# Ranking the activation passes first, and the steps of the next block's x second, in the scheduler's order of ScalarE and VectorE

## The chip, the core and the metric

One core of one Trainium2 chip runs the kernel. A core has TensorE (PE, matmuls; PEld is its weight load), VectorE (DVE), ScalarE (ACT), GpSimd (POOL) and SyncE (SP), whose queue issues every transfer here. Each engine takes its instructions in the order in which they were built into its queue and waits on semaphores for what others make. The metric is the device time of the execution in microseconds.

## The reference, cut to what matters

```python
def phi(x):                                  # attention features, per head, 576 tokens
    proj = x @ w_phi                         # 64 -> 128
    proj = proj - max(abs(proj), axis=-1)
    return concat([exp(proj), exp(-proj)])
kv  = k_p.T @ v;  z = sum(k_p)               # q_p, k_p = phi(q), phi(k)
x   = (q_p @ kv) / (q_p @ z + 1e-6)          # to [4608 tokens, 512]
h   = x @ w_in                               # 512 -> 2048
g   = max(h, 0) + alpha * min(h, 0)
y   = g @ w_out                              # 2048 -> 512
# soft mixture: 32 slots, 8 experts
logits = y @ phi;  d = softmax over tokens;  slots = d.T @ y
out = softmax over slots (logits) @ (relu(slots @ w1) @ w2)
```

All in float32 precision. `w_in` and `w_out` arrive as 64-bit numbers and are turned to float32 on the core.

## The kernel before, in words

The 4608 tokens are 12 blocks n of 384. For each block, 16 chunks c of 128 hidden features: `gemm` (L510 to L523) makes h of the chunk in a PSUM bank with 12 matmuls of 128x384 (L520): x and w_in are each split into a high and a low part, and hi·hi, hi·lo and lo·hi are added for the four pieces of 128 of the inner dimension. In chunk 0 the eight matmuls that read `xhi` come first and the four that read `xlo` last. A bank `ph` is one of two, so the matmuls of chunk c+2 wait until chunk c was read.

`leaky` (L525 to L531) reads it: ScalarE makes relu(-h) into `gT` (L527), VectorE adds alpha_rest times that to h (L528). VectorE then transposes `gT` into `gb` (L547), and for every four chunks TensorE multiplies `gT` with the product of w_out and phi into `pl` (L556). After a block `softmax` takes the logits of the block: `pr` (L575) on TensorE, a maximum, an exponential and transposes on VectorE and ScalarE (L586 to L612), 48 or 96 small matmuls `pS` (L625), and VectorE adds those to `acc` (L644). y itself is never made: its product with the softmax weights is formed from the transposed g. The g of the first two blocks goes to HBM (`gT_d`) and comes back between chunks 4 and 15 of block 10 (`QUADS`, `reload`).

Beside the chunks of block n the attention of block n+1 runs: keys (`pk`, `kall`, `ks`, `pkv`, L269 to L366) and queries (`pq`, `pj`, `mb`, `qe`, `num`, `den`, L394 to L450). `q_finish` (L457 to L494) ends it: `recip` takes 1/den on VectorE (L462, L463) and sends it out and back over HBM so that it is spread over the partitions (L465, L470); `divide` multiplies (L486, four pieces); `scale` makes the two parts of x for the next block, `xhi` on ScalarE (L479) and `xlo` on VectorE (L480), four pieces each. There is one `xhi` and one `xlo`, so the pieces of block n+1 can be written only when the last chunk (15) of block n has read them. `conv` (L174 to L211) turns the weights to float32 until some 270 us.

`at(slot, phase, ...)` puts steps in program order around the chunks (a slot is a chunk). The order in each engine's queue is then made by a scheduler that plays the program through with its own estimate of times: of the instructions that are ready on an engine it takes the one of the highest priority, which is otherwise the place in program order. `tc.high_priority(offset=...)` moves that place ahead for what is issued inside. `combine` (L688 to L704), once per run for the first 28 groups of tokens, is a further row of VectorE passes in block 10.

Of the kernel before, what the change touches and what calls it, by code (L numbers as in the profile page):

```python
# [13 lines left out]
AF = mybir.ActivationFunctionType  # L14
ALU = mybir.AluOpType
# [46 lines left out]
def attention_prelu_softmoe(ctx: ExitStack, tc, qT, kT, v, wphi, w_in, w_out, alpha, phi, w1, w2, out):  # L62
    nc = tc.nc
# [78 lines left out]
    alpha_rest = const.tile([128, NC], F32, name="alpha_rest")  # L142
# [34 lines left out]
    def at(slot, phase, fn):  # L177
        at_step(slot, phase, fn)
# [204 lines left out]
    xhi_t, xlo_t, q_st = {}, {}, {}  # L383
# [73 lines left out]
    def q_finish(slot, n):  # L457
        st = q_st[n]

        def recip():  # L460
            rd = sm.tile([128, BT], F32, tag="dT", name="rd")[:, 0:HB]
            nc.vector.tensor_scalar(out=rd, in0=st["den"][:, 0:HB], scalar1=1e-6, scalar2=None, op0=ALU.add)  # L462
            nc.vector.reciprocal(out=rd, in_=rd)  # L463
            for j in range(2):
                nc.sync.dma_start(rc_d[n % 2][j].rearrange("p h t -> h p t"), rd[64 * j:64 * j + 64])  # L465

        def widen():
            bc = st["bc"] = xp.tile([128, NP, BT], F32, tag="bc", name="bc")
            for j in range(2):
                nc.sync.dma_start(  # L470
                    bc[64 * j:64 * j + 64], rc_d[n % 2][j, 0:NP].rearrange("p h t -> p (h t)").unsqueeze(0).to_broadcast([64, NP, BT]))

        def scale(p):
            def go():
                if p == 0:
                    xhi_t[n] = xp.tile([128, KD, BT], F32R, tag="xhi", name="xhi")
                    xlo_t[n] = xp.tile([128, KD, BT], F32R, tag="xlo", name="xlo")
                xs = st["num"][:, p, :]
                nc.scalar.copy(xhi_t[n][:, p, :], xs)  # L479
                nc.vector.tensor_tensor(out=xlo_t[n][:, p, :], in0=xs, in1=xhi_t[n][:, p, :], op=ALU.subtract)  # L480
            return go

        def divide(p):
            def go():
                xs = st["num"][:, p, :]
                ins = nc.vector.tensor_tensor(out=xs, in0=st["bc"][:, p, :], in1=xs, op=ALU.mult).ins  # L486
                tc.add_manual_dep(ins, mark[max(k for k in mark if k <= slot + 6)].name, nosync, reason="behind the load")
            return go

        at(slot, "post", recip)  # L490
        at(slot + 1, "pre", widen)
        for p in range(NP):
            at(slot + 6, "post", divide(p))
        for p in range(NP):  # L494
            at(slot + 6, "post", scale(p))
# [17 lines left out]
    def gemm(n, c):  # L513
        xhi, xlo = xhi_t[n], xlo_t[n]
        ph = ps_h.tile([128, 512], F32, tag="h", name="ph")
        h = ph[:, 0:BT]
        first = [(k, a, b) for k in range(KD) for a, b in ((0, 0), (1, 0))] + [(k, 0, 1) for k in range(KD)]
        terms = first if c == 0 else [(k, a, b) for k in range(KD) for a, b in ((0, 0), (0, 1), (1, 0))]
        for i, (k, a, b) in enumerate(terms):
            gemm_last[0] = nc.tensor.matmul(  # L520
                h, (w_in_hi, w_in_lo)[a][c][:, 128 * k:128 * k + 128], (xhi, xlo)[b][:, k, :],
                start=(i == 0), stop=(i == len(terms) - 1)).ins
        return h  # L523

    def leaky(n, c, h):  # L525
        gT = gT_t[n, c] = sm.tile([128, 512], F32, tag="gT", name="gT", bufs=5)[:, 0:BT]
        nc.scalar.activation(gT, h, AF.Relu, scale=-1.0)  # L527
        ins = nc.vector.scalar_tensor_tensor(out=gT, in0=gT, scalar=alpha_rest[:, c:c + 1], in1=h, op0=ALU.mult, op1=ALU.add).ins  # L528
        mark[NC * n + c] = ins
        if n < NDEF:  # L530
            nc.sync.dma_start(gT_d[n, c], gT)  # L531
# [216 lines left out]
    for step in range(-45, nslots + 4):  # L748
# [3 lines left out]
        h = None  # L752
        if slot is not None:
            n, c = divmod(slot, NC)
            if 0 <= slot < nslots:
                h = gemm(n, c)
# [5 lines left out]
        if h is not None:  # L762
            leaky(n, c, h)
# [69 lines left out]
    for eg in range(2):  # L833
        for j in range(4):
            nc.vector.tensor_reduce(
                out=own[:, j:j + 1], in_=ident[:, 36 * j + 16 * eg:36 * j + 16 * eg + 4], axis=AX.X, op=ALU.add)
# [3 lines left out]
    for eg in range(2):  # L840
        hr = pf.tile([128, EF], F32, tag=f"hr{eg}", name="hr")
        for fh in range(2):
            pe = ps_h.tile([128, 512], F32, tag="h", name="pe")
            for k in range(KD):
# [3 lines left out]
                out=hr[:, 512 * fh:512 * fh + 512], in0=pe, scalar1=0.0, scalar2=own[:, 4 + eg:5 + eg], op0=ALU.max, op1=ALU.min)  # L848
        t = acc[2 * eg:2 * eg + 2]
        for b in range(2):  # L850
            nc.vector.transpose(
                out=t[b].rearrange("p (b s) -> p b s", s=32),
# [115 lines left out]
```

## Time and profile before

| | |
|---|---|
| median of 3 runs (lowest to highest) | 972.08 us (970.07 to 972.95) |
| profiled execution, its own time | 973.75 us |
| its span, first to last instruction | 971.9 us |
| PE busy | 928.3 us (96%) |
| PEld / DVE / ACT / POOL busy | 654.1 / 722.1 / 443.6 / 143.5 us |
| granted TensorE clock, mean | 0.986 |
| chain of waits, by engine | PE 74%, DVE 17%, DMA 4% |

Busy times are unions over the instructions of an engine; a matmul's recorded time overlaps the next one's, so the start of one to the start of the next is what it costs. In a row of the timeline the brackets give the idle time of the engine ahead of the row and what ended it. The granted clock is 1.00 at 2.4 GHz and 0.50 at 1.2 GHz.

### The profile page before, as it was taken

The page shows a single profiled execution, that of the slowest core. Times are in us where ns is not written, and L with a number is a line of the kernel's source. Part 1 is how long each engine was busy: PE and PEld are TensorE (multiplying, and loading weights), DVE is VectorE, ACT ScalarE, POOL GpSimd, SP SyncE. Part 2 cuts the span into 40 slices and gives each one's busy share as a digit, 9 for nine tenths or more (in the row PEclk, how much of TensorE's full clock was granted, in tenths as well). Part 3 has the DMA queues.
Part 4 walks back from the last instruction along what each step waited for, and adds up shares of the span by engine and source line. Part 5 has one row for each costly group of instructions (what it writes and reads, how often), then busy time and mean ns, then how long its engine had stood idle before and what let it go on. Part 6 is the DMA issues. An engine that isn't in the chain of part 4 may idle for free.

```text
span 971.9 us, 20072 instructions
## 1 busy us (share of the span) xinstructions
PE 928.3 (96%) x8178; PEld 654.1 (67%) x8178; DVE 722.1 (74%) x1425; ACT 443.6 (46%) x867; POOL 143.5 (15%) x84
## 2 busy tenths in 40 slices
PE   6888989999989999999999999999999999899997
PEld 3446676777668676676677776776777667786454
DVE  6998999989686687677677778677756767864233
ACT  5876757766635345245335344353342341221113
POOL 4102212112112112122022112121130220000000
PEclk9898999999999999999999999999999999999999
DMA  7345655674231031031211210200212609478999
GB/s 272 119 141 177 207 169 196 213 203 122 64 87 28 23 85 43 26 78 53 51 44 42 59 53 25 75 26 23 54 34 72 177 1 302 159 268 260 311 354 335
DMA packets 75675, 122.22 MB, mean 126 GB/s; under 512 B 7872, under 2 KB 49472, under 8 KB 75584
## 3 DMA queue, kind: packets, MB, share of 16 engines
q1 hardware_dynamic: 75584, 120.95, 40.3%
q8 instruction: 64, 1.05, 0.5%
q14 instruction: 27, 0.22, 0.1%
HBM read 99.82 MB, written 21.10 MB: 124 GB/s over the span
## 4 chain that ended last, share of the span: by engine, by line
PE 74%; DVE 17%; DMA 4%; issue 2%; ACT 2%; SPq 0%; DVEq 0%; ACTq 0%
PE ph L520 37%; PE num L440 5%; PE pkv L336 5%; PE pS L625 4%; PE pl L556 4%; PE pq L407 3%; PE den L445 3%; PE pk L293 2%; PE pso L866 2%; DVE m L207 2%; DVE gT L528 1%; PE pe L846 1%; DVE mx L281 1%; PE po L902 1%; DVE rest L202 1%
## 5 line engine op out<-in xcount | busy, mean ns | idle before, releaser
L520 PE MATMUL ph<-xhi,w 128*128 128x384 f32 x1536 | 430.8, 351 | 8.2 <-ACT xhi L479 4.0
L520 PEld LDWEIGHTS ph<-xhi,w 128*128 128x128 f32 x1536 | 280.3, 189 | 71.5 <-issue 38.0
L520 PE MATMUL ph<-xlo,w 128*128 128x384 f32 x768 | 257.9, 341 | 0.9 <-DVE xlo L480 0.8
L419 POOL PARTITION_ALL_REDUCE mb<-pj x48 | 137.4, 2864 | 477.4 <-ACT pj L413 326.8
L527 ACT ACTIVATE gT<-ph 128x384 f32<-128x384 f32 x192 | 93.3, 488 | 245.3 <-PE ph L520 239.9
L528 DVE SCALAR_TENSOR_TENSOR gT<-gT,alpha_rest,ph 128x384 f32<-128x384 f32 x192 | 115.7, 604 | 103.8 <-ACT gT L527 102.4
L520 PEld LDWEIGHTS ph<-xlo,w 128*128 128x128 f32 x768 | 144.4, 189 | 9.7 <-issue 4.8
L547 DVE STREAM_TRANSPOSE gb<-gT 128x384 f32<-128x384 f32 x162 | 92.0, 571 | 2.9
L429 ACT ACTIVATE qe<-pj 128x768 f32<-128x768 f32 x90 | 72.2, 839 | 22.9 <-DVE pj L423 14.0
L440 PE MATMUL num<-qe,kv 128*64 128x192 f32 (+1 forms) x488 | 68.6, 411 | 3.5 <-ACT qe L429 3.3
L336 PE MATMUL pkv<-kall 128*64 128x256 f32 x464 | 57.9, 393 | 1.3 <-ACT kall L287 0.7
L281 DVE TENSOR_REDUCE mx<-pk 128x4 f32<-128x512 f32 (+1 forms) x80 | 49.5, 623 | 7.2 <-PE pk L293 5.8
L407 PE MATMUL pq<-qraw,wp 64*128 64x384 f32 x192 | 46.8, 545 | 7.9 <-DMA qraw<-in_qT_dram 4.1
L286 ACT ACTIVATE kall<-kall 128x512 f32<-128x512 f32 x60 | 37.5, 627 | 30.4 <-DVE kall L283 30.2
L440 PEld LDWEIGHTS num<-qe,kv 128*64 128x64 f32 x488 | 31.1, 136 | 27.8 <-issue 18.0
L324 DVE TENSOR_TENSOR ks<-ks,kall 128x256 f32<-128x256 f32 x96 | 47.4, 517 | 0.4
L336 PEld LDWEIGHTS pkv<-kall 128*64 128x64 f32 x464 | 31.6, 140 | 23.5 <-issue 4.8
L423 DVE TENSOR_TENSOR pj<-pj,mb 128x768 f32<-128x768 f32 x48 | 44.8, 932 | 0.0
L283 DVE TENSOR_TENSOR kall<-pk,mx 128x512 f32<-128x512 f32 x60 | 40.8, 680 | 2.2 <-PE pkv L336 1.7
L293 PE MATMUL pk<-wp,kall 64*128 64x128 f32 x512 | 39.5, 293 | 2.9 <-issue 2.6
L293 PEld LDWEIGHTS pk<-wp,kall 64*128 64x128 f32 x512 | 32.9, 194 | 12.8 <-issue 10.8
L413 ACT COPY pj<-pq 128x768 f32<-128x768 f32 x44 | 35.0, 796 | 13.4 <-PE pq L407 13.2
(203 smaller groups left out, 1157.6 us busy)
## 6 DMA issues: line engine op xcount, KB each, us to landing
w<-in_w_dram SPq DMA_DIRECT2D x46, 256.0 KB
kall<-in_v_dram SPq DMA_DIRECT2D x30, 320.0 KB
qraw<-in_qT_dram SPq DMA_DIRECT2D x48, 192.0 KB
bc<-rc_d SPq DMA_DIRECT2D x24, 384.0 KB
out_dram<-os SPq DMA_DIRECT2D x18, 512.0 KB
raw<-in_w_in_dram SPq DMA_DIRECT2D x16, 512.0 KB
raw<-in_w_out_dram SPq DMA_DIRECT2D x16, 512.0 KB
gT_d<-gT SPq DMA_DIRECT2D x32, 192.0 KB
```

The source lines that it names most:

```text
L281: nc.vector.tensor_reduce(out=mx[:, 0:nt], in_=src, axis=AX.X, op=ALU.max, apply_absolute_value=True)
L293: lambda t=t, j=j, sl=slice(64 * j, 64 * j + 64): nc.tensor.matmul(st["pk"][:, j, F * t:F * t + F], st["kraw"][sl, 128 * t:128 * t + 128], ...
L324: nc.vector.tensor_tensor(out=ks[:, j], in0=ks[:, j], in1=f[t], op=ALU.add)
L336: return lambda: nc.tensor.matmul(pkv[64 * j:64 * j + 64, 0:256], st["vt"][:, t, 64 * j:64 * j + 64], part.rearrange("p s f -> p (s f)"), ...
L407: lambda j=j, sl=slice(64 * j, 64 * j + 64): nc.tensor.matmul(pq[j][:, 0:BT], wp[sl, F * j:F * j + F], st["qraw"][sl], start=True, stop=True)
L419: nc.gpsimd.partition_all_reduce(mb, pj, 128, bass_isa.ReduceOp.absmax)
L429: nc.scalar.activation(st["e", s], pj, AF.Exp, scale=(1.0, -1.0)[s])
L440: lambda s=s, j=j: nc.tensor.matmul(num[64 * j:64 * j + 64, o:o + w], kvs[:, s, 64 * j:64 * j + 64], st["e", s][:, j, o:o + w], start=(s = ...
L520: gemm_last[0] = nc.tensor.matmul(h, (w_in_hi, w_in_lo)[a][c][:, 128 * k:128 * k + 128], (xhi, xlo)[b][:, k, :], start=(i == 0), stop=(i = ...
L527: nc.scalar.activation(gT, h, AF.Relu, scale=-1.0)
L528: ins = nc.vector.scalar_tensor_tensor(out=gT, in0=gT, scalar=alpha_rest[:, c:c + 1], in1=h, op0=ALU.mult, op1=ALU.add).ins
L547: nc.vector.transpose(out=half_of(n, c // 8)[:, c % 8, :], in_=gT)
```

## The change

```diff
@@ q_finish
         def recip():
             rd = sm.tile([128, BT], F32, tag="dT", name="rd")[:, 0:HB]
+            with tc.high_priority(offset=2000000):
+                recip_ops(rd)
+
+        def recip_ops(rd):
             nc.vector.tensor_scalar(out=rd, in0=st["den"][:, 0:HB], scalar1=1e-6, scalar2=None, op0=ALU.add)
             nc.vector.reciprocal(out=rd, in_=rd)
...
                 xs = st["num"][:, p, :]
-                nc.scalar.copy(xhi_t[n][:, p, :], xs)
-                nc.vector.tensor_tensor(out=xlo_t[n][:, p, :], in0=xs, in1=xhi_t[n][:, p, :], op=ALU.subtract)
+                with tc.high_priority(offset=2000000):
+                    nc.scalar.copy(xhi_t[n][:, p, :], xs)
+                    nc.vector.tensor_tensor(out=xlo_t[n][:, p, :], in0=xs, in1=xhi_t[n][:, p, :], op=ALU.subtract)
...
-                ins = nc.vector.tensor_tensor(out=xs, in0=st["bc"][:, p, :], in1=xs, op=ALU.mult).ins
+                with tc.high_priority(offset=2000000):
+                    ins = nc.vector.tensor_tensor(out=xs, in0=st["bc"][:, p, :], in1=xs, op=ALU.mult).ins
@@ leaky
-        nc.scalar.activation(gT, h, AF.Relu, scale=-1.0)
-        ins = nc.vector.scalar_tensor_tensor(out=gT, in0=gT, scalar=alpha_rest[:, c:c + 1], in1=h, op0=ALU.mult, op1=ALU.add).ins
+        with tc.high_priority(offset=3000000):
+            nc.scalar.activation(gT, h, AF.Relu, scale=-1.0)
+            ins = nc.vector.scalar_tensor_tensor(out=gT, in0=gT, scalar=alpha_rest[:, c:c + 1], in1=h, op0=ALU.mult, op1=ALU.add).ins
```

No instruction is added or taken away: each engine has the same ones in another order. The two passes of `leaky` now have the highest priority on their engines, and recip, divide, `xhi` and `xlo` the next. The scheduler plays the whole program again, so that TensorE's order changes too. Lines after L461 have larger numbers in the changed kernel (L479, L480, L486 become L484, L485, L492; L520, L527, L528 become L526, L534, L535; L547, L556, L575, L644 become L554, L563, L582, L651).

ScalarE at the change from block 9 to block 10. Before:

```order
L429 ACTIVATE qe<-pj 128x768 x2
L413 COPY pj<-pq 128x768
L479 CAST xhi<-num 128x384 x4
L527 ACTIVATE gT<-ph 128x384
L450 COPY num<-num 128x384 x2
```

ScalarE at the same place now:

```order
L429 ACTIVATE qe<-pj 128x768 x2
L413 COPY pj<-pq 128x768
L534 ACTIVATE gT<-ph 128x384
L484 CAST xhi<-num 128x384 x4
L413 COPY pj<-pq 128x768
```

The relu of chunk 15 stood behind the four `xhi` of the next block and now stands ahead of them; it is so at all eleven changes of block.

TensorE at the change from block 10 (its last chunk reads w_1226) to block 11 (its chunks 0 and 1 read w_615 and w_644). Before:

```order
L520 MATMUL ph<-xlo,w_1226 128x384
L520 MATMUL ph<-xhi,w_1226 128x384
L520 MATMUL ph<-xhi,w_615 128x384 x8
L520 MATMUL ph<-xlo,w_615 128x384 x4
L556 MATMUL pl<-gT,wpr 32x384 x4
L520 MATMUL ph<-xhi,w_644 128x384
```

TensorE at the same place now:

```order
L526 MATMUL ph<-xlo,w_1226 128x384
L526 MATMUL ph<-xhi,w_1226 128x384
L563 MATMUL pl<-gT,wpr 32x384 x4
L526 MATMUL ph<-xhi,w_615 128x384 x2
L526 MATMUL ph<-xhi,w_644 128x384
L526 MATMUL ph<-xhi,w_615 128x384 x6
L582 MATMUL pr<-ls,tident 128x384
```

The four matmuls `pl` of chunks 12 to 15 moved from behind chunk 0 of the new block to ahead of it.

VectorE ahead of the same change of block (cw, cm and logits are `combine`'s, acc and pS the softmax's; the gT rows are the passes of chunks 13, 14 and 15 before, 14 and 15 now). Before:

```order
L702 TENSOR_TENSOR cw<-logits,cm 128x512
L702 TENSOR_TENSOR cw<-logits,cm 128x384
L528 SCALAR_TENSOR_TENSOR gT<-gT,alpha_rest,ph 128x384
L486 TENSOR_TENSOR num<-bc,num 128x384 x4
L704 STREAM_TRANSPOSE logits<-cw 128x512
L704 STREAM_TRANSPOSE logits<-cw 128x384
L547 STREAM_TRANSPOSE gb<-gT 128x384
L528 SCALAR_TENSOR_TENSOR gT<-gT,alpha_rest,ph 128x384
L480 TENSOR_TENSOR xlo<-num,xhi 128x384 x3
L547 STREAM_TRANSPOSE gb<-gT 128x384
L480 TENSOR_TENSOR xlo<-num,xhi 128x384
L528 SCALAR_TENSOR_TENSOR gT<-gT,alpha_rest,ph 128x384
```

VectorE at the same place now:

```order
L709 TENSOR_TENSOR cw<-logits,cm 128x384
L711 STREAM_TRANSPOSE logits<-cw 128x512
L711 STREAM_TRANSPOSE logits<-cw 128x384
L651 SCALAR_TENSOR_TENSOR acc_107<-acc_107,sc,pS 128x512
L651 SCALAR_TENSOR_TENSOR acc_108<-acc_108,sc,pS 128x512
L651 SCALAR_TENSOR_TENSOR acc_109<-acc_109,sc,pS 128x512
L651 SCALAR_TENSOR_TENSOR acc_110<-acc_110,sc,pS 128x512
L535 SCALAR_TENSOR_TENSOR gT<-gT,alpha_rest,ph 128x384
L554 STREAM_TRANSPOSE gb<-gT 128x384
L535 SCALAR_TENSOR_TENSOR gT<-gT,alpha_rest,ph 128x384
L485 TENSOR_TENSOR xlo<-num,xhi 128x384
```

The four passes on `acc` stood ahead of chunk 13's pass and the four divides (L486) behind it; now the divides are further ahead, `combine`'s transposes and all four `acc` passes stand ahead of chunk 14's pass, and chunk 15's pass stands ahead of the first `xlo`.

## Rows read from the trace of the kernel before

**Rows 1.** Stretches: from:to, us, busy us of engines (instructions), granted clock, DMA share, GB/s

```profile
148.00:250.00 102.00, 99.24 (x764) 76.48 (x765) 95.83 (x191) 67.55 (x137) 18.54 (x10) 1.00 0.57 172
250.00:300.00 50.00, 47.45 (x409) 31.19 (x406) 34.24 (x67) 24.82 (x46) 8.42 (x4) 0.97 0.25 69
300.00:800.00 500.00, 499.94 (x4265) 355.29 (x4271) 362.29 (x702) 211.66 (x404) 86.91 (x45) 1.00 0.19 52
800.00:850.00 50.00, 47.19 (x475) 35.25 (x464) 39.34 (x78) 11.56 (x25) 0.00 (x0) 1.00 0.67 221
```

**Rows 2.** TensorE's waits from 148 to 860 us: us in total, times, longest

```profile
PE ph L520 <- DVE gT L528: 2.7, 4, 1.6
PE pkv L342 <- DVE ks L328: 2.4, 1, 2.4
PE ph L520 <- DVE xlo L480: 0.8, 1, 0.8
PE pw L243 <- DVE wpr L250: 0.8, 1, 0.8
```

**Rows 3.** Timeline, start of block 1: start us, us, engine, line, operation, count

```profile
156.30 0.55 DVE L480 TENSOR_TENSOR xlo<-num,xhi 128x384 fp32r<-128x384 f32 x1
...
156.90 0.44 PE L520 MATMUL ph<-xlo,w 128*128 128x384 f32 x1 [0.80 <-DVE xlo L480]
...
158.38 0.55 DVE L480 TENSOR_TENSOR xlo<-num,xhi 128x384 fp32r<-128x384 f32 x1
...
158.54 1.16 PE L293 MATMUL pk<-wp,kall 64*128 64x128 f32 x16
```

**Rows 4.** Timeline, change from block 5 to block 6

```profile
509.87 1.16 PE L293 MATMUL pk<-wp,kall 64*128 64x128 f32 x16
509.97 1.76 ACT L479 CAST xhi<-num 128x384 fp32r<-128x384 f32 x4 [4.54 <-PE ph L520]
510.52 1.50 DVE L480 TENSOR_TENSOR xlo<-num,xhi 128x384 fp32r<-128x384 f32 x3 [1.52 <-ACT xhi L479]
...
510.96 1.66 PE L520 MATMUL ph<-xhi,w 128*128 128x384 f32 x8
```

**Rows 5.** Timeline, behind chunk 10 of block 10

```profile
824.07 0.81 PE L575 MATMUL pr<-ls,tident 128*128 128x384 f32 x2
...
825.32 0.55 DVE L586 TENSOR_REDUCE mbl<-pr 128x1 f32<-128x384 f32 x1
```

**Rows 6.** Timeline, change from block 10 to block 11

```profile
839.26 1.96 DVE L486 TENSOR_TENSOR num<-bc,num 128x384 f32<-128x384 f32 x4
...
841.44 0.34 PE L520 MATMUL ph<-xhi,w 128*128 128x384 f32 x1
...
842.68 0.57 DVE L528 SCALAR_TENSOR_TENSOR gT<-gT,alpha_rest,ph 128x384 f32<-128x384 f32 x1
...
843.40 1.63 PE L520 MATMUL ph<-xhi,w 128*128 128x384 f32 x8 [1.63 <-DVE gT L528]
...
846.17 0.85 PE L556 MATMUL pl<-gT,wpr 128*32 128x384 f32 x8
...
846.95 0.44 PE L520 MATMUL ph<-xhi,w 128*128 128x384 f32 x1
...
847.23 0.34 PE L520 MATMUL ph<-xlo,w 128*128 128x384 f32 x1
```

**Rows 7.** Stretches with TensorE's longer waits, and one behind a wait

```profile
124.00:132.00 8.00, 5.38 (x49) 4.25 (x49) 8.00 (x17) 7.14 (x14) 0.20 (x1) 1.00 0.47 152
272.00:275.60 3.60, 1.16 (x16) 0.21 (x16) 3.60 (x7) 0.89 (x3) 0.00 (x0) 1.00 0.31 91
275.60:279.10 3.50, 3.50 (x17) 3.14 (x18) 2.48 (x5) 1.74 (x3) 0.00 (x0) 0.52 0.10 28
841.00:848.00 7.00, 5.20 (x31) 3.71 (x30) 6.81 (x14) 3.11 (x7) 0.00 (x0) 1.00 0.52 180
```

**Rows 8.** Timeline, SyncE's queue: the last load of the spread reciprocals

```profile
803.54 0.50 SPq L470 DMA_DIRECT2D bc<-rc_d  x1
```

## The prediction

> **What bounds the kernel now.** I read first the table of busy times, where TensorE is busy for 96% of the span, then the windows by stage [rows 1]. The reader is to see three stages there. From 300 to 800 us TensorE is busy for 499.94 of 500 us at full clock, while VectorE has 362.29 and ScalarE 211.66: there is no wait that another order on those two could take away. From 148 to 250 us TensorE stands idle for 102 − 99.24 = 2.76 us with VectorE at 95.83 of 102; from 250 to 300 for 2.55; from 800 to 850 for 2.81. So all that an order of VectorE or ScalarE can win behind 148 us is about 8.2 us.
>
> Then the waits of TensorE in that part [rows 2]. The first matmuls of a chunk wait for VectorE's pass on `gT` four times, 2.7 us together and 1.6 at most; once for `xlo`, 0.8; once for `wpr`, 0.8; and once for `ks`, 2.4. Of these the change touches the first two directly. The longest `gT` wait is the one of 1.63 us at the change from block 10 to 11 [rows 6], so the other three have 2.7 − 1.63 = 1.1 us and lie ahead of 300 us, as the full stretch from 300 to 800 shows.
>
> The orders of ScalarE and VectorE are the same in both kernels up to about 150 us, and again around the `ks` wait and in the tail behind some 862 us. So waits there stay, and so does the half clock (0.52) that follows the `ks` wait for 3.5 us [rows 7].
>
> **The change part by part.** Nothing is added, so the cost is in what each engine now does later. Five terms.
>
> (a) 148 to 250 us. At the start of block 1, two further VectorE passes now stand ahead of the first `xlo` piece and of the last: the `gT` pass of chunk 15, about 0.57 (as in rows 6), and one on `ks`, which I take at no more than that. I take the two as 0.9 us. The matmul that waits for `xlo` waited 0.80 [rows 3] and would wait 1.7. TensorE's keys (L293, 1.16 us [rows 3]) moved from there to behind chunk 0, so the cover that they gave goes too, but they must be done anyway: they fill later time, and what they could fill there was not idle. I add 0.4 for that. Against the +1.3 stand the three `gT` waits, 1.1 us, which the higher rank should end, and half of the `wpr` wait, 0.5, since the chain ahead of it is shuffled. Sum −0.3; bounds +1.3 (none of the waits goes) and −2.7 (`gT`, `xlo` and `wpr` waits all go: 1.1 + 0.8 + 0.8).
>
> (b) TensorE's own order. The matmuls of the gemm stand in 195 unbroken stretches before and in 189 now, other work between them. The first matmul behind such a break costs 847.23 − 846.95 = 0.28 us until the next one starts [rows 6], against some 0.17 for one in the middle, by the row of eight at block 6 (0.17 to 0.21 each [rows 4]). Six breaks fewer at 0.11 are −0.6; bounds −0.9 and −0.3.
>
> (c) The other block changes. At nine of eleven (into blocks 3 to 11) the `pl` matmuls now stand ahead of chunk 0 of the new block, and so TensorE needs chunk 15's relu and `gT` pass before it can go on: about 0.5 on ScalarE (an `xhi` piece of the same shape takes 1.76/4 = 0.44 [rows 4]) and 0.57 on VectorE, with the way between engines 1.2 us. Where keys or queries stand between, they cover it. At block 6 the cover is the keys alone, 510.96 − 509.87 = 1.09 us [rows 4]; 1.2 − 1.09 = +0.1. On the other side the four `xhi` come one relu later, but the `xhi` of block 6 had waited 4.54 us for TensorE, and the first eight matmuls still start only when TensorE is free. Bounds 0 and, if one more pass stands ahead of `gT` at each, +5.4 (a rival below).
>
> (d) Block 11. Here VectorE is the late one, with no keys or queries left as cover. The `pr` matmuls of the previous softmax (824.07 [rows 5]) now stand behind chunk 11 instead of chunk 10, one gemm or 12 × 0.174 = 2.1 us later. From the reduction that reads them (825.32 [rows 5]) to the `gT` pass of chunk 14, which ends at about 843.2 [rows 6], VectorE has 17.9 us of passes with nearly no gaps. In the changed order the same number of passes (four on `gT`, four transposes into `gb`, the softmax, `combine`, the divides at 1.96 us [rows 6], four on `acc`) lies between that reduction and the pass of chunk 15. So this one ends at 827.4 + 17.3 to 17.9 = 844.8 to 845.3. TensorE is through with chunk 15 at about 841.7 [rows 6] and now waits for that pass, not for chunk 14's: some 3.5 us against 1.63. Then come `pl`, 846.95 − 846.17 = 0.78, and chunk 0, 12 × 0.174 = 2.1, so that both are done at about 848.0 to 848.2, where they were at 846.95. That is +1.1; bounds +0.6 and +1.7.
>
> The rank could have been thought to help here, since `gT` stands first. What is ahead of it in VectorE's order is not, however, overtaken at run time: the trace has the four divides and both transposes of `combine` between two `gT` passes while TensorE waits [rows 6]. The Trainium skill (PSUM — Partial Sum Buffer, Engine vs sequencer instructions) says that the queues of ScalarE and VectorE are strict first in, first out; the trace agrees, with a `gT` pass 842.68 behind a divide that began at 839.26. If it were not so, chunk 15's pass would end near 842.7 and this term would be about −1.3.
>
> (e) The clock behind that wait. A wait of 2.4 us at 272 was followed by a granted clock of 0.52 for 3.5 us; waits of 2.6 us (8 − 5.38) spread from 124 to 132 and of 1.63 at 841 were not, at 1.00 in both stretches [rows 7]. One of 3.5 us is longer than any of these, so I take a fall for likely: 3.5 us at half speed lose 3.5 × 0.48 = 1.7 us; bounds 0 and twice that, 3.4. The Trainium skill (TensorE: Matmul & The Clock Gate, What's actually happening) says that throttled is the default and that activity releases it, which goes with the row at 272; by that alone the fall is sure to come where the wait is long enough, and the sum stays as it is.
>
> What costs nothing: the load of the spread reciprocals for block 11 now stands behind the reloads of `gT_d` on SyncE's queue, but it was issued at 803.54 [rows 8] and first used at 839.26 [rows 6], 35 us of cover; without it each us would lengthen (d).
>
> Sum: −0.3 − 0.6 + 0.1 + 1.1 + 1.7 = +2.0 us. The profiled execution took 973.75 (span 971.9 and 1.85 around it), so 975.75 for it; that execution stood 1.67 above the median of 972.08, which becomes 974.1.
>
> **Rivals.**
>
> B: the reordering is worth nothing and the clock does not fall: −0.3 − 0.6 + 0.1 + 1.1 = +0.3, 972.4 us. For it: 1.63 us at 841 left the clock alone. Against: the longer wait.
>
> C: the rank does what its name says, and every wait for `gT`, `xlo` and `wpr` behind 148 us goes: −2.7 − 0.8 − 0.8 − 0.6 = −4.9, 967.2 us; with the `ks` wait and its half clock (2.4 + 1.7) it would be 963.1. For it: VectorE has the room on average. Against: its order ahead of block 11, where `combine` and `acc` still stand ahead of `gT`, and the unchanged rows around `ks`.
>
> D: slower, by `pl` ahead of the new block's first gemm. If in the real run one more VectorE pass (0.57 to 0.6) is in progress or queued ahead of chunk 15's `gT` pass, the chain is 1.8 us instead of 1.2 and passes the cover at each of the nine changes: 9 × 0.6 = 5.4, and with +0.3 the time is 977.8. It decides from the point at which the chain is longer than what stands between chunk 15 and `pl`, 1.09 us at block 6. For it: that cover is so thin there. Against: at most other changes there are more matmuls between, and the rank puts `gT` ahead of the other passes that are ready.
>
> **How the numbers follow.** A, the forecast, 0.40, its own range 972.6 to 975.6; B 0.22; C 0.18; D 0.20. A difference of 0.3%, 2.9 us, is about what a measurement of this kernel can tell from no change: faster is below 969.2, slower above 975.0. C gives nearly all of faster, and B little: 0.19. Slower is D, 0.20, and the part of A above 975.0, where the clock falls twice or the wait is longer, 0.13: 0.33. The rest, 0.48, is no change. The range goes from 967.5 (near C) to 978.5 (a little over D).
>
> **What would show it.** Right: the wait at the change into block 11 names `gT`, is some 3.5 us long and ends near 845, and the granted clock behind it is about half for 3.5 us; the `xlo` wait at block 1 is near 1.7 us; the three `gT` waits between 148 and 300 are gone; 300 to 800 stays full; the `ks` wait stays at 2.4. Wrong: a wait into block 11 under 2 us, or idle time of TensorE at the block changes between 300 and 800, which would be D.

## The result and the profile after

The changed kernel takes 979.96 us (median of 5 runs, 976.92 to 980.74); the kernel before took 972.54 us (median of 5, 970.07 to 973.53). The ratio is 1.0075, with a 95% interval of 1.0054 to 1.0096: slower by 7.4 us. The forecast was 974.1 with a range up to 978.5, counted from the 972.08 of the first three runs, so the sign was right and the size was not. One of the twelve executions of e3 below took 1740.75 us; its ratio leaves that one out, and its median of 975.67 becomes 975.55 without it.

The profiled execution after took 979.96 us with a span of 978.2, against 973.75 and 971.9. TensorE is busy for 931.5 us (928.3 before), VectorE for 728.1 (722.1). First the stretches, as in [rows 1]; columns: from:to, us, busy us of PE, PEld, DVE, ACT, POOL (instructions), granted clock, DMA share, GB/s. Then three stretches at the change from block 10 to block 11.

```profile
148.00:250.00 102.00, 97.93 (x759) 76.03 (x761) 96.69 (x191) 67.19 (x137) 19.65 (x10) 1.00 0.56 174
250.00:300.00 50.00, 47.44 (x412) 30.92 (x409) 34.05 (x67) 24.58 (x46) 8.43 (x4) 0.97 0.24 69
300.00:800.00 500.00, 499.66 (x4227) 354.93 (x4239) 365.62 (x700) 212.62 (x405) 88.00 (x45) 1.00 0.18 52
800.00:850.00 50.00, 44.22 (x493) 31.99 (x462) 39.76 (x77) 10.58 (x23) 0.00 (x0) 0.96 0.65 202
...
842.50:847.20 4.70, 0.03 (x1) 0.00 (x0) 4.67 (x9) 2.12 (x5) 0.00 (x0) 0.86 0.99 313
847.20:851.80 4.60, 4.57 (x18) 3.33 (x19) 2.31 (x5) 0.48 (x1) 0.00 (x0) 0.50 0.35 124
847.20:852.70 5.50, 5.47 (x20) 3.92 (x20) 2.31 (x5) 0.48 (x1) 0.00 (x0) 0.50 0.45 159
```

TensorE's idle time rose from 2.8 to 4.1 us between 148 and 250, and from 2.8 to 5.8 between 800 and 850. In the middle it is still busy for all but 0.34 of 500 us. At the change into block 11 it stands still for 4.7 us while VectorE is busy for 4.67 of them, and then works for 5.5 us at a granted clock of 0.50, which by that clock costs half of the stretch, 2.7 us.

TensorE's waits from 148 to 863 us, as in [rows 2]: us in total, times, longest.

```profile
PE pl L563 <- DVE gT L535: 4.7, 1, 4.7
PE pkv L342 <- DVE ks L328: 2.4, 1, 2.4
PE pw L249 <- ACT sw L245: 1.3, 1, 1.3
PE ph L526 <- DVE gT L535: 1.2, 3, 0.7
PE ph L526 <- DVE xlo L485: 0.9, 1, 0.9
PE pl L563 <- DMA gT<-gT_d: 0.8, 1, 0.8
PE pS L632 <- DVE logits L619: 0.7, 1, 0.7
PE ph L526 <- ACT xhi L484: 0.5, 1, 0.5
```

The `ks` wait did not move. The `gT` waits did not go: besides the one of 4.7 us there are three of 1.2 us together, where three of 1.1 stood beside the one of 1.63. The `wpr` wait went, and four waits of other names are new: `sw`, the reload of `gT_d`, `logits` and `xhi`. The large one, in the timeline (start us, us, engine, line, operation; in brackets the idle time ahead and what ended it), to be held against [rows 5, 6]:

```profile
828.94 0.61 DVE L535 SCALAR_TENSOR_TENSOR gT<-gT,alpha_rest,ph 128x384 f32<-128x384 f32 x1 [0.85 <-ACT gT L534]
829.47 0.55 DVE L593 TENSOR_REDUCE mbl<-pr 128x1 f32<-128x384 f32 x1
...
841.77 1.16 DVE L711 STREAM_TRANSPOSE logits<-cw 128x512 f32<-128x512 f32 x2
...
842.19 0.34 PE L526 MATMUL ph<-xhi,w 128*128 128x384 f32 x1
842.57 0.49 ACT L534 ACTIVATE gT<-ph 128x384 f32<-128x384 f32 x1 [1.60 <-PE ph L526]
842.86 2.69 DVE L651 SCALAR_TENSOR_TENSOR acc<-acc,sc,pS 128x512 f32<-128x512 f32 x4
...
845.46 0.61 DVE L535 SCALAR_TENSOR_TENSOR gT<-gT,alpha_rest,ph 128x384 f32<-128x384 f32 x1
846.11 0.58 DVE L554 STREAM_TRANSPOSE gb<-gT 128x384 f32<-128x384 f32 x1
846.61 0.57 DVE L535 SCALAR_TENSOR_TENSOR gT<-gT,alpha_rest,ph 128x384 f32<-128x384 f32 x1
...
847.23 1.50 PE L563 MATMUL pl<-gT,wpr 128*32 128x384 f32 x8 [4.70 <-DVE gT L535]
...
856.38 1.15 PE L632 MATMUL pS<-gb,d 32*32 32x512 f32 x32 [0.74 <-DVE logits L619]
```

From the reduction that reads `pr` to the end of chunk 15's pass VectorE works, with one gap of 0.41 us, for 847.18 − 829.47 = 17.7 us. TensorE's part beside it, from 829.47 to the end of chunk 15 at 842.53, lasts 13.06. The difference, 4.65 us, is the wait but for the 0.05 between `gT` and `pl`. Chunk 15's relu was done at 843.06, but the four `acc` passes and chunk 14's pass stand ahead of its `gT` pass in VectorE's queue; it began at 846.61, behind them.

Where the 6.3 us of span go can be read from the last matmul of a block in the two traces. Block 2 ends at 306.74 before and 307.19 after, block 9 at 780.16 and 782.11, block 10 at 841.44 and 842.19, block 11 at 885.11 and 891.83:

```profile
306.74 0.34 PE L520 MATMUL ph<-xhi,w 128*128 128x384 f32 x1
...
780.16 0.34 PE L520 MATMUL ph<-xhi,w 128*128 128x384 f32 x1
...
885.11 0.34 PE L520 MATMUL ph<-xhi,w 128*128 128x384 f32 x1
```

```profile
307.19 0.34 PE L526 MATMUL ph<-xhi,w 128*128 128x384 f32 x1
...
782.11 0.34 PE L526 MATMUL ph<-xhi,w 128*128 128x384 f32 x1
...
891.83 0.34 PE L526 MATMUL ph<-xhi,w 128*128 128x384 f32 x1
```

So up to block 2 the loss is 0.45 us, in blocks 3 to 9 another 1.5 (474.92 against 473.42). Block 10 gives 1.2 back (60.08 against 61.28), block 11 takes 6.0 more (49.64 against 43.67), and the rest of the program 0.5 less.

### The profile page after: what moved, and what is told of

Its sections match the earlier page's. It is cut to its first block, busy times and chain, and to the rows that moved or that the text cites. A ratio compares the mean times of both kernels' runs of the same rounds, so it can differ in the third digit from the quotient of the medians.

```text
span 978.2 us, 20065 instructions
## 1 busy us (share of the span) xinstructions
PE 931.5 (95%) x8178; PEld 655.8 (67%) x8178; DVE 728.1 (74%) x1425; ACT 444.1 (45%) x867; POOL 145.2 (15%) x84
## 4 chain that ended last, share of the span: by engine, by line
PE 67%; DVE 5%; DMA 1%; ACT 1%; issue 1%; SPq 0%; DVEq 0%; ACTq 0%
PE ph L526 33%; PE num L440 5%; PE pkv L336 4%; PE pS L632 4%; PE pl L563 3%; PE pq L407 3%; PE den L445 3%; PE pk L293 2%; PE pso L873 2%; PE pe L853 1%; PE po L909 1%; PE idle L108 1%; PE pt L358 1%; PE spin L108 1%; DVE gT L535 1%; DMA gT<-gT_d 1%
## 5 line engine op out<-in xcount | busy, mean ns | idle before, releaser
L526 PE MATMUL ph<-xhi,w 128*128 128x384 f32 x1536 | 427.3, 350 | 7.3 <-ACT xhi L484 3.9
L526 PEld LDWEIGHTS ph<-xhi,w 128*128 128x128 f32 x1536 | 280.3, 190 | 71.0 <-issue 38.5
L526 PE MATMUL ph<-xlo,w 128*128 128x384 f32 x768 | 254.6, 341 | 0.9 <-DVE xlo L485 0.9
L534 ACT ACTIVATE gT<-ph 128x384 f32<-128x384 f32 x192 | 93.5, 489 | 243.4 <-PE ph L526 241.2
L535 DVE SCALAR_TENSOR_TENSOR gT<-gT,alpha_rest,ph 128x384 f32<-128x384 f32 x192 | 115.7, 604 | 116.8 <-ACT gT L534 116.0
L526 PEld LDWEIGHTS ph<-xlo,w 128*128 128x128 f32 x768 | 143.7, 189 | 11.0 <-issue 7.3
L554 DVE STREAM_TRANSPOSE gb<-gT 128x384 f32<-128x384 f32 x162 | 92.0, 571 | 2.9
L281 DVE TENSOR_REDUCE mx<-pk 128x4 f32<-128x512 f32 (+1 forms) x80 | 49.6, 625 | 6.9 <-PE pk L293 6.2
L407 PE MATMUL pq<-qraw,wp 64*128 64x384 f32 x192 | 49.1, 564 | 4.8 <-DMA qraw<-in_qT_dram 3.8
L563 PE MATMUL pl<-gT,wpr 128*32 128x384 f32 x336 | 38.6, 505 | 5.8 <-DVE gT L535 4.7
L324 DVE TENSOR_TENSOR ks<-ks,kall 128x256 f32<-128x256 f32 x96 | 41.6, 455 | 0.4
```

Of the source, the lines that this page charges most:

```text
L281: nc.vector.tensor_reduce(out=mx[:, 0:nt], in_=src, axis=AX.X, op=ALU.max, apply_absolute_value=True)
L407: lambda j=j, sl=slice(64 * j, 64 * j + 64): nc.tensor.matmul(pq[j][:, 0:BT], wp[sl, F * j:F * j + F], st["qraw"][sl], start=True, stop=True)
L526: gemm_last[0] = nc.tensor.matmul(h, (w_in_hi, w_in_lo)[a][c][:, 128 * k:128 * k + 128], (xhi, xlo)[b][:, k, :], start=(i == 0), stop=(i = ...
L554: nc.vector.transpose(out=half_of(n, c // 8)[:, c % 8, :], in_=gT)
L563: lambda g=g: nc.tensor.matmul(pl_t[n][32 * g:32 * g + 32, :], wpr[:, c - 3 + g, :], gT_t.pop((n, c - 3 + g)), start=(c == 3), stop=(c == ...
```

## The experiments

Each was timed beside the kernel before on the same chip; its median there was 972.2 to 972.8 us in all four sessions. Two theories stood against each other at first. T: VectorE's order at the end of block 10 makes the loss. R: every block change pays a little.

**Each rank alone.** In e1 the two passes of `leaky` keep their rank and the steps of x lose it; in e2 it is the other way round.

```diff
@@ e1: recip, xhi and xlo, divide
-                with tc.high_priority(offset=2000000):
@@ e2: leaky
-        with tc.high_priority(offset=3000000):
```

> Only the two passes of leaky have their rank; recip, divide, xhi and xlo stand as before. Theory T: the loss is made by the rank of leaky, chiefly at the change from block 10 to 11, where VectorE's fixed order has combine and the four acc passes ahead of the gT passes of chunks 14 and 15; here that order is the same, so TensorE waits there 3.5 to 5 us again with the granted clock near 0.5 behind it, and the time is 976 to 981 us. Rival R: the loss is spread over all eleven block changes, by both ranks; then this kernel has about half of it, 975 to 977, and the wait into block 11 is under 3 us.

> Only recip, divide, xhi and xlo have their rank; leaky stands as before. Theory T: nothing is lost, 970 to 974 us, and the wait into block 11 stays at 1 to 2.5 us. Rival R: about half of the loss, 975 to 977.

Measured: e1 979.01 us, ratio 1.0066 (1.0048 to 1.0084); e2 975.92, 1.0035 (1.0023 to 1.0047). e1 has the wait (3.68 us, then 0.43 more), as T says. Not all of its loss is there, however: near 170 us it waits 3.06 us for `sw` (1.28 in the changed kernel), with the clock at 0.50 for 6.4 us behind it. And e2, with a wait of only 1.63 us there, loses 3.3 us, which T did not expect and R did. Its trace shows only a part of that: the profiled execution was its fastest, 974.23 us, with a span 0.3 us over that of before. In it the `ks` wait is gone, and block 2 ends 2.5 us earlier; between the ends of blocks 2 and 9 it needs 781.34 − 304.26 = 477.08 us, 3.7 more than before, and from 300 to 800 us TensorE is idle for 0.23 us in all.

```profile
304.26 0.34 PE L526 MATMUL ph<-xhi,w 128*128 128x384 f32 x1
...
781.34 0.34 PE L526 MATMUL ph<-xhi,w 128*128 128x384 f32 x1
```

So the 3.7 us are hardly waiting. Sixteen more matmuls of the keys stand in that stretch (the row below, of before and then of e2, from block 2's end to block 9's), 16 × 0.07 = 1.1 us that were done earlier before. The rest is the same matmuls in another order: in e2's trace TensorE goes from one kind of matmul (by the tile that it writes) to another 344 times there, against 331 before.

```profile
L293 PE MATMUL pk<-wp,kall 64*128 64x128 f32 x240 | 17.9, 285 | 0.0
```

```profile
L293 PE MATMUL pk<-wp,kall 64*128 64x128 f32 x256 | 18.6, 285 | 0.0
```

What makes e2's median 1.7 us longer than its profiled execution no trace shows. The two losses do not add: 6.4 + 3.3 is more than the 7.4 of both ranks together.

**Combine later.** In e3 (on the changed kernel) and e5 (on the kernel before) the first call of `combine` is issued seven chunks later.

```diff
-    at(NC * (NB - 1) - 3, "post", lambda: combine(0, NT - 8))
+    at(NC * (NB - 1) + 4, "post", lambda: combine(0, NT - 8))
```

> The whole change, with the first call of combine issued seven chunks later, in block 11 instead of block 10. Theory T: the wait of 4.7 us into block 11 falls under 1 us, the half clock behind it goes, and the time is 971 to 975 us (979.96 less 4.7, less 2.3 for the half clock, and up to 0.7 for the wait on logits). Rival R: the place of combine plays no part in what the other block changes cost, and the time stays at 977 to 980.

> The kernel before, with the same move of combine. Theory T: its own wait of 1.63 us into block 11 goes, 970 to 972 us. Rival: what combine leaves in block 10 comes back as waits in block 11, 972 to 975.

Measured: e3 975.67 us, 1.0032 (1.0018 to 1.0046), between the two ranges of its expectation; e5 971.15, 0.998 (0.9968 to 0.9991). The wait of e3 is still 2.29 us, where T expected less than 1:

```profile
845.56 0.85 PE L563 MATMUL pl<-gT,wpr 128*32 128x384 f32 x8 [2.29 <-DVE gT L535]
```

The reason is in VectorE's rows. The scheduler pulled combine's first five VectorE passes back into block 10, and only the two products and the two transposes left it. These took 842.86 − 840.70 = 2.16 us in the changed kernel, from the first product to the first `acc` pass, and 4.70 − 2.29 = 2.41 is what the wait lost: the queue from the reduction to chunk 15's pass is 15.3 us in e3 where it was 17.7. In e3 the clock behind the wait is 1.00. About 3 us of the loss stay.

**Where pl stands.** e4 ties `pl` behind chunk 0 of block 11 (and four matmuls of chunk 1) by one added matmul, VectorE's order up to there as it was. Block 10's `pr` and `pS` go back with it, behind chunks 2 and 4.

```diff
+            if (n, c) == (NB - 2, NC - 1):
+                before = spin(1, gemm_last[0])
```

> The whole change; at the change from block 10 to 11 alone one extra matmul ties the pl matmuls so that they stand behind chunk 0 of block 11 and four matmuls of chunk 1, with all of VectorE's order as in the changed kernel. Theory T (VectorE is late with both gT passes): chunk 0 still waits, now for chunk 14's pass, which ended 1.1 us ahead of chunk 15's; the wait is 3 to 4 us and the time 977.5 to 979.5. Rival P (the place of pl ahead of chunk 0 makes the loss): the wait falls to under 2 us as before the change, and the time to 974 to 976.

Measured: 979.07 us, 1.0073 (1.0058 to 1.0088), a wait of 3.67 us. Rival P falls: chunk 0 needs the bank of chunk 14, whose pass stands behind the same `acc` passes.

**Which blocks.** e6 ranks only in blocks 0 and 1 (x of blocks 0 to 2), e7 everywhere else.

```diff
-        with tc.high_priority(offset=3000000):
+        with (tc.high_priority(offset=3000000) if n < 2 else ExitStack()):    # e6; e7: n >= 2
```

The steps of x have their condition in the same way (e6: n < 3; e7: n >= 3).

> The ranks stand only in blocks 0 and 1 (leaky) and for the x of blocks 0 to 2; from block 3 on the order of VectorE is that of before. Theory T: this part costs what the traces show as idle time of TensorE between 148 and 300 us, 1.3 to 2 us: 973.5 to 975. Rival: nothing, within a microsecond of 972.6, and the idle time is the difference of one run from another.

> The ranks stand everywhere but in the first two blocks; up to block 1 the order is that of before, and at the change into block 11 that of the changed kernel. Theory T: the wait into block 11 of 4 to 5 us, and the half clock behind it, stay, and with them 4.5 to 6.5 us of the loss: 977 to 979. Rival: under half of the loss, below 976.

Measured: e6 972.97 us, 1.0007 (0.9996 to 1.0019); e7 978.97, 1.0067 (1.005 to 1.0084), with the wait of 4.69 us. The first blocks cost 0.7 us by the ratio, from −0.4 to +1.8 by its interval. The median lies where the rival had it, within a microsecond of 972.6: T's 1.3 to 2 us for e6 is not confirmed, though the interval does not exclude it.

**pr earlier.** e8 ranks the copy `ls` and the `pr` matmul of block 1's softmax first, half a chunk's gain.

```diff
+            with tc.high_priority(offset=4000000 if n == 1 else 0):
                 pl_read[n].append(nc.scalar.copy(ls, pl_t.pop(n)).ins)
```

> The whole change, with the copy ls and the pr matmul of block 1's softmax ranked first, which puts pr in the middle of chunk 11 of block 10 instead of behind it, 1.0 us earlier; nothing else moves by much. Theory T (all VectorE passes from the reduction of pr to chunk 15's gT pass are one queue of fixed length, 17.7 us): the wait falls by 0.8 to 1.1 us, to about 3.7, and the time to 977 to 979, or 975 to 977 if the half clock goes too. Rival: the wait is set by something later in the queue and does not move, 979 to 981.

Measured: 978.09 us, 1.006 (1.0046 to 1.0074). The wait is 3.87 us, 0.83 less, as T says, but not by a queue of fixed length: from the reduction (826.98) to the end of chunk 15's pass (845.47) it is 18.5 us, as one more `gT` pass fell behind the reduction, and TensorE's part beside it is 14.7 instead of 13.06. The difference still is the wait. The half clock stays for 3.5 us; the two stretches are the wait and what follows it:

```profile
841.60:845.50 3.90, 0.06 (x1) 0.00 (x0) 3.87 (x8) 2.12 (x5) 0.00 (x0) 0.97 1.00 317
845.50:849.00 3.50, 3.47 (x15) 2.23 (x16) 2.31 (x5) 0.48 (x1) 0.00 (x0) 0.54 0.20 70
```

**Combine tied behind.** e9 (on the changed kernel) and e10 (on the kernel before) add an order to the later issue, so that nothing of combine is pulled back. e11 is e9 with the ranks in the middle blocks alone.

```diff
+        ins = nc.vector.tensor_reduce(out=c, in_=lg, axis=AX.X, op=ALU.max).ins
+        tc.add_manual_dep(ins, mark[NC * (NB - 1) + 1].name, nosync, reason="behind block 10")
@@ e11 besides
+        with (tc.high_priority(offset=3000000) if 2 <= n < NB - 2 else ExitStack()):
...
+                with (tc.high_priority(offset=2000000) if 3 <= n < NB - 1 else ExitStack()):
```

> The whole change, with the first call of combine not only issued later but tied behind chunk 1 of block 11, so that all of its passes leave VectorE's order ahead of block 11 (moving the issue alone left four of them there and the wait at 2.29 us). TensorE's order is that of the changed kernel. Theory T: the queue from the reduction of pr to chunk 15's gT pass shortens by 5.7 to 6 us, to about 12, less than TensorE's 13 us beside it, so that only the plain way through relu and the gT pass is left, a wait of 1 to 1.4 us; full clock behind it; 973 to 975 us. Rival: a wait over 2 us stays at that place whatever VectorE has ahead, 975.5 or more.

> The kernel before with the same tie. Theory T: its wait of 1.63 us into block 11 (0.60 where the issue alone was moved) falls to 0.5 or less, 970 to 971.5 us. Rival: combine's passes, now beside the last softmax, hold up block 11 itself, 971.5 to 973.

> Combine tied behind as in the two kernels beside it; leaky ranked in blocks 2 to 9 alone, the x steps for blocks 3 to 10 alone. Against the kernel before with the tie this prices the middle of the program by itself. Theory T: TensorE's middle part is never idle, and what its new order costs there is what the traces show from the end of block 2 to the end of block 9, +0.7 to +1.5 us: 971 to 973. Rival D (pl ahead of the new block's gemm waits at each change): 5 us more, 975 to 977.

Measured: e9 978.78 us, 1.006 (1.0046 to 1.0073), far over the 973 to 975 of T; e10 970.5, 0.9978 (0.9967 to 0.9988); e11 970.79, 0.9978 (0.9968 to 0.9988), a little under its range. The wait of e9 did fall to 1.23, with full clock behind it, and still the time hardly moved. Its rows tell a part of why:

```profile
844.57 0.85 PE L563 MATMUL pl<-gT,wpr 128*32 128x384 f32 x8 [1.23 <-DVE gT L535]
...
851.20 3.39 PE L632 MATMUL pS<-gb,d 32*32 32x512 f32 x96 [0.76 <-DVE logits L619]
...
861.28 0.44 PE L526 MATMUL ph<-xhi,w 128*128 128x384 f32 x1 [2.30 <-DVE gT L535]
```

```profile
858.01 2.69 DVE L651 SCALAR_TENSOR_TENSOR acc<-acc,sc,pS 128x512 f32<-128x512 f32 x4
860.62 0.61 DVE L535 SCALAR_TENSOR_TENSOR gT<-gT,alpha_rest,ph 128x384 f32<-128x384 f32 x1
```

The changed order asks for block 10's softmax at once behind the change of block: `pr` inside chunk 0 and `pS` behind chunk 1, where before they stood in chunk 2 and behind chunk 4. Combine, moved to block 11, met that softmax there, and the same picture (combine and `acc` ahead of a `gT` pass) came back 17 us later, with 2.30 us. Block 11, from the end of block 10 to its own, is 3.4 us shorter than in the changed kernel (46.23 against 49.64); in the profiled runs the stretches ahead of it and behind it take 1.8 of that back, and no run shows why. The theory was right about the place and wrong to expect the time back. In e10 nothing of this comes: its softmax stands further off, its only wait there is 0.60 for `xhi` (0.5 or less was expected). And e11 needs 780.11 − 305.94 = 474.17 us for the middle, 0.75 more than before, which its block 10 gives back (no wait on VectorE there, and a shorter `pS`).

**Both remedies, and the last blocks alone.** e12 is e9 with e4's tie. e13 ranks `leaky` in blocks 10 and 11 and the x of block 11 only, with combine in its old place.

```diff
-        with tc.high_priority(offset=3000000):
+        with (tc.high_priority(offset=3000000) if n >= NB - 2 else ExitStack()):    # e13
```

> The whole change with both remedies at once: combine tied behind chunk 1 of block 11, and the pl matmuls of block 10 tied behind chunk 0 of block 11 (which also puts block 10's pr back behind chunk 2 and its 48 pS behind chunk 5). Either alone gave little, since the wait of 4.70 us came back as 3.67 (pl alone) or as 1.23, 0.76 and 2.30 (combine alone). Theory T2: the end of block 10 is lost twice over, by combine ahead of the gT passes and by a softmax that TensorE now asks for earlier than VectorE can serve it; with both gone no wait over 1 us is left from 840 to 880 us and the time is 971 to 974 us. Rival: what the ranks cost ahead of block 10 is more than the parts measured alone, 975 or more.

> The ranks stand only for leaky in blocks 10 and 11 and for the x of block 11; everything ahead is the order of before, and so TensorE keeps pr behind chunk 10 and pS behind chunk 12 of block 10. Theory T2: the ranks do not lose time by what they put first there, but by how the shifted play-through of all blocks ahead of it had placed pr, pS and pl; so the wait stays near 1.6 us and the time is 972 to 973.5 us. Rival: the ranks at the end are enough, 976 or more.

Measured: e12 975.86 us, 1.0037 (1.0026 to 1.0049); e13 973.69, 1.0012 (0.9999 to 1.0024). e13 is near no change, just over its range, with a wait of 1.65 as before: T2 holds in that the ranks of the last blocks alone do not make the loss. What the ranks ahead did to the place of `pr`, `pS` and `pl` is needed too. T thus accounts for block 11; for the 1.5 us of blocks 3 to 9, which no remedy there took away, it does not. e12 misses T2's range: the second wait is gone, but at the block change stands another,

```profile
847.59 1.84 PE L526 MATMUL ph<-xhi,w 128*128 128x384 f32 x9 [1.80 <-ACT xhi L484]
```

1.80 us for `xhi`, which in e10 was 0.60: with chunk 0 directly behind chunk 15, ScalarE's relu of chunk 15 stands between, and so does its way. From the end of block 10 to the end of block 11 e12 needs about what before needed (43.8 and 43.7 us), and so does e13 (43.9). With one remedy alone it was 47.8 (e4) and 46.2 (e9), and 49.6 in the changed kernel: so the 6.0 us of block 11 are `combine` ahead of the `gT` passes and the early softmax together. What e12's profiled run still loses lies ahead: 3.05 us by the end of block 2, where the clock behind the `ks` wait is 0.50 from 277.3 to 283.6 (for 3.5 us before), and 1.5 us in blocks 3 to 9, as in the changed kernel. Block 10, with a wait of 1.5 us on a reload of `gT_d` in it, takes no more than before (60.8 and 61.3).

## Why the prediction was wrong

**What bounds the kernel** held: TensorE, full from 300 to 800 us, and the end of block 10 as the one place where VectorE is late.

**Rival D** (a wait at nine changes) is refuted: 0.34 us of idle time from 300 to 800. The time came out above D's 977.8, but not by D. **Rival C** is refuted by VectorE's queue, as argued. In **B** neither half held.

**(a)**, forecast −0.3: the idle time between 148 and 250 rose by 1.3 us, the upper bound, in the profiled run; by e6 the price of these blocks is 0.7 (−0.4 to +1.8). The `xlo` wait is 0.86, not 1.7, and the `wpr` wait went, but the three `gT` waits stayed and `sw` (1.3) and `xhi` (0.5) came new: what was put first made something else late.

**(b)**, forecast −0.6, is the step that failed by most: blocks 3 to 9 cost +1.5, and with the +0.1 of (c) that is 2.0 us off. I priced each break in the gemm alike and counted only those. A tally of the two traces from block 2's end to block 9's puts the cost at the changes of kind: from one start to the next they take 97.28 us in all against 95.96, though there are 333 and 331 of them, while the steps between matmuls of one kind take 377.64 against 377.45. Of the 1.3 us, 0.28 is new idle time. So which kinds stand next to each other counts, and not only how many changes there are; which pairs cost what is not worked out, and no run was made for it.

**(c)**, forecast +0.1 at block 6: `pl` starts 0.14 us behind the keys (512.39 to 512.53). Right. That the relu ahead of `xhi` is free was right only where other matmuls stand between (e12).

**(d)**, forecast +1.1 with a wait of 3.5 us: the wait was mis-sized, the price was not. The queue from the reduction to chunk 15's pass was forecast at 17.3 to 17.9 us and is 17.7. The error is on the other side of the subtraction: I let TensorE finish chunk 15 at its old time and moved only the reduction. But TensorE's stretch between the two became shorter by more than the one gemm: the 96 `pS` took 834.24 − 829.05 = 5.19 us before, with a pause of 0.66 in them, and 838.08 − 834.13 = 3.95 after. That is 1.24 us, and 3.5 + 1.2 is the 4.70 measured. But this made nothing later: TensorE came to the meeting point 1.2 us earlier and waited that much longer for the same pass. At full clock `pl` and chunk 0 would have been done at 847.23 + 0.78 + 2.1 = 850.1, 3.2 us behind 846.95; 1.95 of these were lost ahead of block 10, so (d) itself is +1.2. (By the forecast's own terms its lower end would have been 844.8 + 0.78 + 2.1 = 847.7, not 848.0.) What was missing is a further 0.74, the wait of `pS` on `logits`, which was not in the sum: I had not followed the softmax of block 10 past the change of block.

```profile
829.05 1.90 PE L625 MATMUL pS<-gb,d 32*32 32x256 f32 x83
...
832.92 1.38 PE L625 MATMUL pS<-kall,d 32*32 32x256 f32 x52 [0.66 <-issue]
834.24 0.85 PE L556 MATMUL pl<-gT,wpr 128*32 128x384 f32 x8
```

```profile
834.13 1.91 PE L632 MATMUL pS<-gb,d 32*32 32x256 f32 x82
...
838.08 0.44 PE L526 MATMUL ph<-xhi,w 128*128 128x384 f32 x1
```

**(e)**, forecast 1.7: the clock fell as forecast, but for 5.5 us at 0.50 instead of 3.5, which is 2.7 us. Its bound of 3.4 holds.

**Costs nothing**: the spread reciprocals were not waited for, as forecast. But `pl` waited 0.8 us for a reload of `gT_d`, and 1.1 to 1.9 us in e3, e4, e7, e8, e9 and e12. The last reload is issued at 815.71 in the changed kernel (810.64 before), 5.1 us later, where the block began 1.95 later; no run moved it.

In all: forecast +2.0. In the profiled runs 0.45 until the end of block 2 (forecast −0.3), 1.5 in blocks 3 to 9 (−0.5), 1.2 for (d) (+1.1), 2.7 for (e) (+1.7) and 0.74 for the wait that was put at nothing: 6.6, where the spans differ by 6.3 and the medians by 7.4. So the place, the cause and the price of the wait were right; TensorE's own order (b) was mis-sized by 2.0 us, the clock by 1.0, the first blocks by 0.75, and the second wait was left out.

## What to carry to other kernels

A rank in a scheduler changes more than what it names: it re-plays the whole program, and most of the loss here came from the other steps (`pr`, `pS`, `pl`) that it set in another place. Where two engines run side by side to a meeting point, forecast both lengths after the change, never one after and one before, and take the price from when the later side arrives, not from how long the other waits. And look at the next thing that is due behind a wait before counting its removal as a gain: e9 took away 3.5 us of waiting and met 2.3 of it again 17 us later. The version that beats both kernels leaves the ranks out and ties combine behind the change of block, e10: 970.5 us, 0.22% under before (0.12 to 0.33); e5 and e11 cannot be told from it.

## What the hardware showed

With the instructions in the same order the middle of the program repeats to a few hundredths: 474.92, 474.93, 474.91, 474.87 and 474.90 us from the end of block 2 to that of block 9 in the changed kernel, e4, e8, e9 and e12; 473.42, 473.42, 473.36 and 473.41 in the kernel before, e5, e10 and e13. The clock behind a wait does not: the `ks` wait of 2.4 us near 273 was followed by 0.52 in the kernel before and by 1.00 in e5, with nothing changed up to there. The row of e5 over the stretch that [rows 7] show at 0.52:

```profile
275.60:279.10 3.50, 2.37 (x19) 2.10 (x20) 3.50 (x7) 1.29 (x3) 0.00 (x0) 1.00 0.10 29
```

At the change into block 11 it fell in part or whole behind 3.67, 3.68, 3.87, 4.69 and 4.70 us of waiting, and not behind 1.23, 1.63, 1.80 and 2.29. Yet in e4 it fell near 826 behind a wait of 1.90, to 0.67 on the mean of this stretch:

```profile
824.30:829.50 5.20, 4.94 (x22) 4.25 (x23) 2.71 (x6) 0.87 (x2) 0.00 (x0) 0.67 1.03 323
```
